# Attention and two expert layers on one core: four value blocks in place of six, queries loaded one pair of blocks later

## The chip, the cores and the metric

The kernel runs on one core of a Trainium2 chip. The core has a matmul engine (TensorE, PE in the profile; its weight loads are PEld), a vector engine (VectorE, DVE), a scalar engine (ScalarE, ACT), GpSimd (POOL) and a synchronisation engine (SyncE, SP), which here does nothing but issue DMA transfers. Sixteen DMA engines move data between the chip's DRAM and the on-chip memory SBUF. All engines run at the same time and wait for each other by semaphores.

The metric is the device time of one execution in microseconds (us), lower is better. Before the change it is 724.68 us, the median of three runs (722.94 to 727.16).

## The reference

Three layers follow one another. First, attention over 4 sequences of 576 tokens with 8 heads of 64; four heads see the last 32 tokens, the other four see every fourth of the last 128:

```python
rel = pos[:, None] - pos[None, :]
mask_plain = (rel >= 0) & (rel < window)                                             # window 32
mask_dil = (rel >= 0) & (rel < window * dilation) & (rel % dilation == 0)            # dilation 4
scores = np.where(masks[None], scale * np.matmul(q, k.transpose(0, 1, 3, 2)), -1e9)
attn = np.exp(scores - np.max(scores, axis=-1, keepdims=True))
out = np.matmul(attn / (np.sum(attn, axis=-1, keepdims=True) + 1e-09), v)
```

Then a layer of 8 experts: each of the 2304 tokens goes to the expert with the largest logit, which computes `relu(x @ w1[e]) @ w2[e]`, scaled by two gates. Last, a dense layer: `h = relu(x @ w_in)`, `out = (h * h) @ w_out`.

## The kernel before, in words

The kernel has three stages on the one core. Attention takes about the first 89 us, the experts the next 260, the dense layer the rest. The change lies in attention alone.

Attention goes over 18 blocks of 128 tokens. For each block it multiplies queries and keys into scores (`qk`, matmuls of line 454), adds the mask and takes the maximum on VectorE (lines 468 and 474), subtracts it on GpSimd (line 475), takes the exponential on ScalarE (line 480), transposes the result on PE (`tr`, line 487), copies it (line 489), multiplies it with the values (`pv`, line 503), normalises on VectorE (lines 513 to 521) and transposes the block for the gate's logits (`xt`, line 540). Blocks are gathered in five groups; at a group's end its logits and its routing lists are computed (lines 563 to 672), and its rows are stored to DRAM (`x_d`, lines 531 and 534). From the eleventh block on, the lists of the first three groups are known, the largest expert is chosen, and its weights (line 141) and tokens are loaded while attention's last blocks run.

The order of the work is written out by hand. In iteration i of the loop over blocks, PE gets `tr(i)`, `qk(i + 2)`, `xt(i - 1)` and `pv(i)`, in that order, and the loads for later blocks are issued between them from SyncE. Each engine takes its instructions in program order, and so does SyncE with its DMA issues, each of which first waits for its buffer to be free (and for a semaphore that one of the eight transfers before it held).

Three kinds of input stream into attention. A load of queries (`load_q`, line 366) brings a pair of blocks into one of three buffers. A load of keys (`load_k`, line 373) brings one to three blocks into a ring of five. A load of values (`load_v`, line 383) brings a pair of blocks into a ring `vb` of VR = 6 blocks; since each load fills only every second partition of each half, the rest of a buffer is set to zero once, by `clear_v` (line 393), one half on VectorE and one on GpSimd. `clear` (line 428) sets the routing lists in DRAM to zero.

Before the loop, queries of blocks 0 to 3, keys of blocks 0 to 4 and values of blocks 0 and 1 are loaded, then queries 4 and 5 and values 2 and 3. In iteration 0, values 4 and 5 follow.

Of the kernel before, what the change touches and what calls it, by code (L numbers as in the profile page):

```python
# [25 lines left out]
NB = NT // P  # L26
# [29 lines left out]

VN = 16 * (D + 1)
VL = -(-2 * VN // 128) * 128
VR = 6
KW = (LAP + 1) * 4 * P + 3 * P  # L60


# [9 lines left out]
def attention_experts_kernel(ctx: ExitStack, tc: tile.TileContext, qB, kB, vB, wE, wF, consts, late, rows, out):  # L72
    nc = tc.nc
# [43 lines left out]
    def loaded(ap, engine, n, why):  # L117
        _, vals = nc.values_load_multi_w_load_instructions(
            ap, engines=[engine], min_val=0, max_val=n, skip_runtime_bounds_check_because=why
        )  # L120
        return vals
# [17 lines left out]
    def load_w(r, c, queue="e"):  # L139
        t = raw_tile()  # L140
        QUEUE[queue].dma_start(out=t, in_=wE[ds(reg[queue, r], 1), c].rearrange("a p n -> p (a n)"))
        raw_t[r, c] = t

    def conv_h(r, c):
        w_t[r, c] = free.pop(0)
        nc.scalar.copy(out=slots[w_t[r, c]][:, 0], in_=raw_t[r, c])  # L146
# [22 lines left out]
    def gather(w):  # L169
        known = (NB if w else EARLY) * P  # L170
        for i, n in tiles(w):
            t = stg.tile([P, DM], F32, tag="xg", name="xg", bufs=4)
            nc.gpsimd.indirect_dma_start(  # L173
                out=t[:n], out_offset=None, in_=x_d[0:known],
                in_offset=bass.IndirectOffsetOnAxis(ap=mt[:n, w, i, 0:1].bitcast(U32), axis=0),
                bounds_check=known - 1, oob_is_err=False,
            )
            xg_t[w, i] = t
# [164 lines left out]
    def attention():  # L343
# [9 lines left out]
        kz = kf[:, :, 0:(LAP + 1) * 4 * P].rearrange("p h (t a s) -> p h t a s", t=LAP + 1, a=4)  # L353
        vb = c2.tile([P, 2, VR, 4, 4, D + 1], F32, name="vb")
        q_t = {}
# [7 lines left out]
        def load_q(i, n):  # L363
            q = wk.tile([P, 2, 4, P], F32, tag="q", name="q", bufs=3)
            a = i % 2
            nc.sync.dma_start(out=q[:, 0:n].rearrange("p i a s -> p (i a s)"), in_=qB[i // 2, :, a:a + n].rearrange("p i s -> p (i s)"))
            for j in range(n):
                q_t[i + j] = q[:, j]

        def load_k(i, n, engine=nc.sync):  # L370
            t = i % LAP
            for h2 in range(2):
                engine.dma_start(out=kf[h2:P:2, h2, 4 * P * (t + 1):4 * P * (t + 1 + n)], in_=kB[h2, :, 4 * P * i:4 * P * (i + n)])

        def wrap():

            nc.scalar.copy(out=kz[:, :, 0, 0:2, 96:P], in_=kz[:, :, LAP, 0:2, 96:P])
            nc.scalar.copy(out=kz[:, :, 0, 2:4], in_=kz[:, :, LAP, 2:4])

        def load_v(i, n, engine=nc.sync):  # L380
            j = i % VR
            for h2 in range(2):
                engine.dma_start(
                    out=vb[h2:P:2, h2, j:j + n].rearrange("p i a c e -> p (i a c e)"),
                    in_=vB[i // 2, h2, :, VN * (i % 2):VN * (i % 2 + n)],
                )
# [5 lines left out]
        def clear_v(j, h2, engine):  # L392
            engine.memset(vb[:, h2, j], 0.0)
# [27 lines left out]
        def load_consts():  # L421
            nc.sync.dma_start(out=late_sb, in_=late)
            nc.sync.dma_start(out=rowc, in_=rows)
# [3 lines left out]
        def clear():  # L427
            nc.sync.dma_start(
                out=meta_d.rearrange("(p a n) c -> p a (n c)", p=P, a=4), in_=z.unsqueeze(1).to_broadcast([P, 4, MS * E * MR // P // 4])
            )  # L430
# [6 lines left out]
        def qk(i):  # L437
            qk_mm(i)
            qk_x(i)
# [37 lines left out]
        def ex(i):  # L477

            pr = wk.tile([P, 4, 64, 2], F32, tag="pr", name="pr")
            nc.scalar.activation(out=pr.rearrange("p a m h -> p a h m"), in_=sm_t.pop(i).rearrange("p (a h) m -> p a h m", h=2), func=ACTF.Exp, scale=0.125)  # L480
            p_t[i] = pr

        def tr(i):
            pr = p_t.pop(i)
            ps = ps_1.tile([P, 4, P], F32, tag="pt", name="pt")
            for p in range(4):
                nc.tensor.transpose(ps[:, p, :], pr[:, p].rearrange("p m h -> p (m h)"), ident)
            pt = wk.tile([P, 4, P], F32, tag="pts", name="pts")
            nc.scalar.copy(out=pt, in_=ps)
            pt_t[i] = pt  # L490

        def pv_mm(i, apart=False):
# [4 lines left out]
            else:  # L497
                t = ps_1.tile([P, 4, 256], F32, tag="o", name="o")
                o = [t[:, 0:2], t[:, 2:4]]
            v = vb[:, :, i % VR]  # L500
            for p in range(4):
# [166 lines left out]
        def scatter(g, cols=None):  # L668
            di, m, _ = rt[g]
            n = rows_of(g)  # L670
            for b in cols or range(COLS[g]):
                ins = nc.gpsimd.indirect_dma_start(
                    out=meta_d, out_offset=bass.IndirectOffsetOnAxis(ap=di[n, b:b + 1].bitcast(U32), axis=0),
                    in_=m[n, b, :], in_offset=None, bounds_check=E * MS - 1, oob_is_err=False,
                ).ins
                for o in scat:
                    tc.declare_no_dep(ins, o, reason="each slot of a list is written once")
                scat.append(ins)
# [8 lines left out]
        nc.gpsimd.memset(z.rearrange("p (n c) -> p n c", c=MR)[:, :, 2:3], OOB)  # L687
        nc.gpsimd.memset(idw, 0)
        ex(0)
        load_q(4, 2)  # L690
        load_v(2, 2)
        warm(7)
        ends = {g[-1] + 1: n for n, g in enumerate(GROUPS)}
# [14 lines left out]
        for i in range(NB):  # L708
            tr(i)
            if i + 1 < NB:  # L710
                ex(i + 1)
            if i == NB - 3:
                gather(0)
            if i + 2 < NB:
                qk(i + 2)
            t = (i + 2) % LAP
            n = i + 2 - t + LAP
            if t == 2 and n < NB:
                load_k(n, 2)
            if t == 4 and n + 2 < NB:  # L720
                wrap()
                load_k(n + 2, min(3, NB - n - 2))

            if i % 2 == 0 and i + 6 < NB:
                load_q(i + 6, 2)
            if i == 0:
                load_consts()
            if i == 3:
                clear()
            if i == 3:  # L730
                nc.vector.tensor_copy(tri, tri32)
                nc.vector.tensor_copy(idw[:, :, :, 0:4], idsb)
                nc.vector.tensor_copy(cs[:, 0, :], io8)
            for a, g in ((2, ends.get(i - 2)), (4, ends.get(i - 3))):
                if g is not None and g < FIRST:
                    scatter(g, range(a - 2, min(a, COLS[g])))
            if i == EARLY + 2:
                reg["e", 0] = loaded(e0_t, SPE, E - 1, PERM)[0]
                load_w(0, 0)
                meta_load(0, nc.sync, "e")  # L740
                load_w(0, 1)
            if i == EARLY + 3:
                load_w(0, 2)
            if i > 0:
                xt(i - 1)
            if i == NB - 3:
                conv_h(0, 0)
            if i == NB - 1:
                transposes0()
            g = ends.get(i - 1)  # L750
            if g == FIRST:
                cnt = route4(g)
            pv_mm(i)
            if g is not None and g != FIRST:
                route4(g)
            if i == NB - 1:
                route5(NG - 2)
                scatter(NG - 2)
                route6(NG - 2)
                splits0()  # L760
                lg_block(i - 1)
            pv_x(i)
            if i == NB - 2:
                scale(0)
            if i == NB - 1:
                conv_w(0, 1)
            if i == 0:
                for j in range(4, VR):
                    clear_v(j, 0, nc.vector)
                    clear_v(j, 1, nc.gpsimd)  # L770
                load_v(4, 2)
            if i % 2 == 1 and i + VR - 1 < NB:
                load_v(i + VR - 1, 2)
            if i in STORES:
                store(STORES[i])
            if i in ends:
                lg(ends[i])
                route1(ends[i])
                route2(ends[i])
                route3(ends[i])  # L780
            if i == NB - 3:
                conv_l(0, 0)
                load_w(0, 3)
            if g is not None and g < NG - 2:
                route5(g)
                if g == FIRST:
                    scatter(g)
                    choose(wk, cnt)
                route6(g)
                if g == FIRST:  # L790
                    first_part(wk)
            if i == NB - 2:
                lg_block(i - 1)
                store(NG - 2)
# [889 lines left out]
```

## Time and profile before

| | before |
|---|---|
| median of 3 runs | 724.68 us (722.94 to 727.16) |
| the profiled execution | 724.47 us, span 722.8 us |
| PE busy | 694.7 us, 96% of the span |
| VectorE, ScalarE, GpSimd busy | 486.4, 326.5, 114.5 us |
| granted clock of PE | 0.998 of full speed |

The span is the time from the first to the last instruction; a little lies around it. Busy times are of one profiled execution. Idle time of an engine is put down to whatever ended it: another engine's instruction, a DMA, or "issue", where the engine waited for nothing that the profile shows.

### The profile page before, as it was taken

Reading aid. Unit: us, or ns where it says so; the run is one execution under the profiler, and the core shown is the slowest. Engines: PE = TensorE matmul, PEld = TensorE weight load, DVE = VectorE, ACT = ScalarE, POOL = GpSimd, SP = SyncE. Lnnn points to the kernel's source line nnn. Section 1 sums busy time; section 2 is a strip of 40 time slices with the busy share of each in tenths; the row PEclk is TensorE's granted clock in tenths of the full one; section 3 lists DMA queues with packets and bytes.
Section 4 is the critical chain, followed back from the end, with each engine's and each line's share of the span. In section 5 each row is a group of like instructions: output and inputs, shape, how many; then the busy total and the mean of one; then the engine's idle time right before and its main releaser. Section 6 shows DMA issues by size and latency. Waiting matters only on the chain.

```text
span 722.8 us, 13818 instructions
## 1 busy us (share of the span) xinstructions
PE 694.7 (96%) x5203; PEld 631.9 (87%) x5203; DVE 486.4 (67%) x878; ACT 326.5 (45%) x599; POOL 114.5 (16%) x120
## 2 busy tenths in 40 slices
PE   7988889999999999989999999999999999999995
PEld 4766789999999999989999999999988888888884
DVE  7866775773646567668886878787889854445441
ACT  2443544543455555556555545565534422122120
POOL 6245336202010110008000000000000040012003
PEclk9999999999999999999999999999999999999999
DMA  8999556865475776862657545556755453235302
GB/s 281 414 338 316 183 165 210 261 182 162 157 221 158 229 239 190 245 203 64 219 165 249 194 152 195 193 203 231 238 170 196 139 177 108 91 119 162 110 22 91
DMA packets 65503, 138.11 MB, mean 191 GB/s; under 512 B 12838, under 2 KB 40023, under 8 KB 64407
## 3 DMA queue, kind: packets, MB, share of 16 engines
q1 hardware_dynamic: 53538, 121.60, 51.9%
q0 software_dynamic: 3984, 10.22, 4.1%
q10 hardware_dynamic: 7909, 5.35, 2.3%
q8 instruction: 43, 0.70, 0.4%
q14 instruction: 29, 0.24, 0.1%
HBM read 102.06 MB, written 35.12 MB: 190 GB/s over the span
## 4 chain that ended last, share of the span: by engine, by line
PE 68%; issue 10%; DVE 2%; DMA 2%; POOL 1%; ACT 1%; ACTq 0%; POOLq 0%; DVEq 0%; SPq 0%
PE op L1489 6%; PE op L1490 6%; PE op L1491 6%; PE bank_b L881 5%; PE bank_b L879 4%; PE bank_b L880 4%; PE yp L879 4%; PE yp L880 4%; PE hp L879 4%; PE yp L881 4%; PE hp L880 4%; PE hp L881 4%; PE bank_d L881 2%; PE bank_d L880 2%; PE bank_d L879 2%
## 5 line engine op out<-in xcount | busy, mean ns | idle before, releaser
L1454 DVE TENSOR_TENSOR slot_d<-gq,slot_d 128x768 fp32r<-128x768 f32 x48 | 45.9, 957 | 63.8 <-ACT slot_d L1452 62.3
L1452 ACT CAST slot_d<-gq 128x768 fp32r<-128x768 f32 x48 | 40.0, 835 | 95.2 <-PE op L1490 83.1
L1499 POOL DMA_INDIRECT out<-os,idc x18 | 20.0, 1112 | 352.9 <-DVE os L1498 348.3
L893 ACT ACTIVATE hh<-hp 128x240 fp32r<-128x240 f32 (+5 forms) x72 | 29.2, 410 | 42.3 <-PE hp L881 40.4
L1445 DVE SCALAR_TENSOR_TENSOR gq<-gq 128x768 f32<-128x768 f32 x48 | 45.7, 952 | 2.1 <-DMA gq<-g_d 2.1
L173 POOL DMA_INDIRECT xg<-x_d,mt x24 | 25.7, 1069 | 135.2 <-PE xp L197 123.2
L150 DVE TENSOR_TENSOR slot_d<-raw,slot_d 128x1024 fp32r<-128x1024 f32 x24 | 29.2, 1223 | 20.6 <-ACT slot_d L146 20.1
L1489 PE MATMUL op<-slot_b,slot_d 128*128 128x512 f32 x108 | 42.0, 389 | 0.0
L1490 PE MATMUL op<-slot_b,slot_d 128*128 128x512 f32 x108 | 42.0, 389 | 0.0
L1489 PE MATMUL op<-slot_a,slot_d 128*128 128x512 f32 x108 | 42.0, 389 | 0.0
L1490 PE MATMUL op<-slot_a,slot_d 128*128 128x512 f32 x108 | 42.0, 389 | 0.0
L1491 PE MATMUL op<-slot_a,slot_d 128*128 128x512 f32 x108 | 42.0, 389 | 0.0
L1491 PE MATMUL op<-slot_b,slot_d 128*128 128x512 f32 x108 | 42.0, 389 | 0.0
L894 DVE SCALAR_TENSOR_TENSOR hl<-hp,hh 128x240 fp32r<-128x240 f32 (+5 forms) x72 | 31.5, 449 | 14.8 <-ACT hh L893 12.1
L914 ACT COPY ys<-yp 128x240 f32<-128x240 f32 (+5 forms) x36 | 14.4, 399 | 48.8 <-PE yp L881 42.5
L880 PE MATMUL yp<-hl,slot_b 128*128 128x240 f32 (+3 forms) x112 | 31.8, 284 | 0.3 <-DVE hl L894 0.3
L879 PE MATMUL yp<-hh,slot_b 128*128 128x240 f32 (+3 forms) x112 | 32.1, 286 | 0.0
L150 DVE TENSOR_TENSOR slot_b<-raw,slot_b 128x1024 fp32r<-128x1024 f32 x20 | 24.2, 1220 | 11.4 <-ACT slot_b L146 11.0
L881 PE MATMUL yp<-hh,slot_b 128*128 128x240 f32 (+3 forms) x112 | 31.7, 283 | 0.0
L879 PE MATMUL hp<-xh,slot_d 128*128 128x432 f32 (+3 forms) x96 | 30.5, 318 | 0.3 <-DVE hl L894 0.3
L880 PE MATMUL hp<-xl,slot_d 128*128 128x432 f32 (+3 forms) x96 | 30.2, 315 | 0.0
L881 PE MATMUL hp<-xh,slot_d 128*128 128x432 f32 (+3 forms) x96 | 30.2, 314 | 0.0
(338 smaller groups left out, 2277.5 us busy)
## 6 DMA issues: line engine op xcount, KB each, us to landing
raw<-in_wE SPq DMA_DIRECT2D x64, 512.0 KB
g_d<-cr SPq DMA_DIRECT2D x96, 192.0 KB
gq<-g_d SPq DMA_DIRECT2D x48, 384.0 KB
raw<-in_wF SPq DMA_DIRECT2D x32, 512.0 KB
vb<-in_vB SPq DMA_DIRECT2D x16, 520.0 KB
yr<-yT_d SPq DMA_DIRECT2D x16, 384.0 KB
q<-in_qB SPq DMA_DIRECT2D x8, 512.0 KB
kf<-in_kB SPq DMA_DIRECT2D x8, 256.0 KB
```

Of the source, the lines that this page charges most:

```text
L150: nc.vector.tensor_tensor(out=lo, in0=raw_t.pop((r, c)), in1=hi.bitcast(F32), op=ALU.subtract)
L879: nc.tensor.matmul(out=out, lhsT=wh, rhs=mh, start=first, stop=False, skip_group_check=shared)
L880: nc.tensor.matmul(out=out, lhsT=wh, rhs=ml, start=False, stop=False, skip_group_check=shared)
L881: nc.tensor.matmul(out=out, lhsT=wl, rhs=mh, start=False, stop=last, skip_group_check=shared)
L893: nc.scalar.activation(out=h[:, :n], in_=p[:, :n], func=ACTF.Relu)
L894: nc.vector.scalar_tensor_tensor(out=l[:, :n], in0=p[:, :n], scalar=0.0, in1=h[:, :n].bitcast(F32), op0=ALU.max, op1=ALU.subtract)
L1445: nc.vector.scalar_tensor_tensor(out=x, in0=x, scalar=0.0, in1=x, op0=ALU.max, op1=ALU.mult)
L1452: nc.scalar.copy(out=h, in_=x)
L1454: return lambda: nc.vector.tensor_tensor(out=l, in0=x, in1=h.bitcast(F32), op=ALU.subtract)
L1489: nc.tensor.matmul(out=o_t[j], lhsT=h[:, a], rhs=w[:, 0], start=f == 0, stop=False)
L1490: nc.tensor.matmul(out=o_t[j], lhsT=h[:, a], rhs=w[:, 1], start=False, stop=False)
L1491: nc.tensor.matmul(out=o_t[j], lhsT=l[:, a], rhs=w[:, 0], start=False, stop=f == 15)
```

## The change

The ring of values holds four blocks in place of six. Values 4 and 5 are no longer loaded in iteration 0 into buffers of their own, whose four clearing memsets go; they come in iteration 1 into the buffers of blocks 0 and 1. Every later pair of values comes in the same iteration as a pair did before, but it is the pair before that one, and one more load stands in iteration 13 (values 16 and 17). Queries go the same way: the load ahead of the loop goes, iteration i (even) loads the pair from i + 4 in place of i + 6, and iteration 12 has one more load (queries 16 and 17).

```diff
-VR = 6
+VR = 4
...
         ex(0)
-        load_q(4, 2)
         load_v(2, 2)
         warm(7)
...
-            if i % 2 == 0 and i + 6 < NB:
-                load_q(i + 6, 2)
+            if i % 2 == 0 and i + 4 < NB:
+                load_q(i + 4, 2)
...
-            if i == 0:
-                for j in range(4, VR):
-                    clear_v(j, 0, nc.vector)
-                    clear_v(j, 1, nc.gpsimd)
-                load_v(4, 2)
             if i % 2 == 1 and i + VR - 1 < NB:
                 load_v(i + VR - 1, 2)
```

The order of SyncE's issues at the start of the loop, before (`q` queries, `vb` values, `kf` keys, `late_sb` and `rowc` constants; partitions x elements of 4 bytes, `x2` two transfers):

```order
L383 DMA vb<-in_vB 64x1040 x2
L366 DMA q<-in_qB 128x1024
L383 DMA vb<-in_vB 64x2080 x2
L373 DMA kf<-in_kB 64x1024 x2
L366 DMA q<-in_qB 128x1024
L422 DMA late_sb<-in_late 128x400
L423 DMA rowc<-in_rows 1x128
L383 DMA vb<-in_vB 64x2080 x4
```

The same place after the change:

```order
L383 DMA vb<-in_vB 64x1040 x2
L383 DMA vb<-in_vB 64x2080 x2
L373 DMA kf<-in_kB 64x1024 x2
L366 DMA q<-in_qB 128x1024
L422 DMA late_sb<-in_late 128x400
L423 DMA rowc<-in_rows 1x128
L383 DMA vb<-in_vB 64x2080 x2
L373 DMA kf<-in_kB 64x1536 x2
L366 DMA q<-in_qB 128x1024
```

The first query load of the loop, which holds blocks 6 and 7 before, holds 4 and 5 after, and it is the only load of these two blocks; one pair of values is left out of the line, and keys 7 to 9 and queries 6 and 7 follow it.

SyncE's issues around iterations 12 and 13 after the change, as the difference to before (`raw` weights of the first expert, `x_d` the store of a group, `ISA` a register instruction):

```order
 L383 DMA vb<-in_vB 64x2080 x2
 L373 DMA kf<-in_kB 64x512 x2
+L366 DMA q<-in_qB 128x1024
 L531 DMA x_d<-x 128x3x256
 L534 DMA x_d<-x 32x3x256 x4
@@ -47,4 +47,5 @@
 L141 ISA
 L141 DMA raw<-in_wE 128x1024
+L383 DMA vb<-in_vB 64x2080 x2
 L141 ISA
 L141 DMA raw<-in_wE 128x1024
```

The added queries stand ahead of the third group's store, and the added values between the second and third weight loads. On PE nothing moves; on VectorE and GpSimd only the memsets of line 393 after block 0 are gone.

## Rows read from the trace of the kernel before

**Rows 1.** The first page: busy us of PE; DMA engines' busy tenths in 40 slices.
```profile
PE 694.7 (96%) x5203; PEld 631.9 (87%) x5203; DVE 486.4 (67%) x878; ACT 326.5 (45%) x599; POOL 114.5 (16%) x120
...
DMA  8999556865475776862657545556755453235302
```

**Rows 2.** Chain of waits, its beginning: start us, us, what.
```profile
102.64 0.97 POOL meta_d L672
...
110.37 4.69 DMA xg<-x_d,mt
...
115.70 0.32 PE xp L197
```

**Rows 3.** Timeline of PE, 0 to 40: start, us, instruction, count [idle before].
```profile
7.66 1.08 PE L454 MATMUL s<-kf,q 128*32 128x128 f32 x32 [0.56 <-DMA q<-in_qB]
...
11.78 0.63 PE L487 MATMUL pt<-ident,pr 128*128 128x128 f32 x4 [1.42 <-DMA ident<-in_consts]
...
13.60 1.09 PE L503 MATMUL o<-vb,pts 128*32 128x130 f32 x32 [0.18 <-DMA vb<-in_vB]
...
19.17 1.08 PE L454 MATMUL s<-kf,q 128*32 128x128 f32 x32
...
26.01 1.08 PE L454 MATMUL s<-kf,q 128*32 128x128 f32 x32
...
31.28 1.08 PE L454 MATMUL s<-kf,q 128*32 128x128 f32 x32 [0.36 <-DMA kf<-in_kB]
...
38.20 1.05 PE L503 MATMUL o<-vb,pts 128*32 128x130 f32 x26 [1.52 <-issue]
```

**Rows 4.** Timeline of SyncE's issues, 0 to 23 us.
```profile
4.07 0.59 SPq L366 DMA_DIRECT2D q<-in_qB  x1
...
6.96 0.43 SPq L410 DMA_DIRECT2D ident<-in_consts  x1
...
15.77 1.35 SPq L366 DMA_DIRECT2D q<-in_qB  x1
...
22.06 1.48 SPq L373 DMA_DIRECT2D kf<-in_kB  x2
```

**Rows 5.** DMA issues by line, with KB each.
```profile
vb<-in_vB SPq DMA_DIRECT2D x16, 520.0 KB
q<-in_qB SPq DMA_DIRECT2D x8, 512.0 KB
...
kf<-in_kB SPq DMA_DIRECT2D x8, 256.0 KB
```

**Rows 6.** Windows: us, PE busy (instructions), PE's clock, DMA share, GB/s.
```profile
13.60:31.28 17.68, 15.86 (x356) 1.00 1.02 407
...
36.00:38.00 2.00, 0.69 (x9) 1.00 1.01 400
42.00:43.00 1.00, 1.00 (x25) 1.00 0.43 164
...
43.30:61.44 18.14, 16.91 (x377) 1.00 0.98 335
61.44:69.46 8.02, 7.29 (x151) 1.00 1.00 326
77.00:82.00 5.00, 4.23 (x76) 1.00 0.81 296
```

**Rows 7.** Timeline of VectorE and GpSimd: the memsets of iteration 0.
```profile
16.10 1.87 POOL L393 MEMSET vb<- 128x1040 f32 x2
16.17 0.93 DVE L393 MEMSET vb<- 128x1040 f32 x1 [0.17 <-issue]
```

**Rows 8.** Timeline of PE, 61 to 89 us.
```profile
61.44 0.91 PE L454 MATMUL s<-kf,q 128*32 128x128 f32 x23
...
69.46 0.41 PE L454 MATMUL s<-kf,q 128*32 128x128 f32 x5
...
82.91 1.09 PE L503 MATMUL o<-vb,pts 128*32 128x130 f32 x32 [0.69 <-ACT pts L489]
...
88.97 0.38 PE L879 MATMUL hp<-xh,slot_a 128*128 128x240 f32 x1
```

**Rows 9.** Timeline of SyncE, the second and third weight load.
```profile
75.57 0.88 SPq L141 DMA_DIRECT2D raw<-in_wE  x2
```

## The prediction

> **What bounds the kernel now.** The first page says that the matmul engine is the bound: PE is busy 96% of the span, in every slice but the first and last, while the DMA engines are full only in the first slices and fall to half later [rows 1]. The chain of waits comes next. It begins where attention's last lists leave for DRAM, and runs through the gather of the first expert's tokens into that expert's transposes on PE [rows 2]. So what attention loses is not made up behind it: experts and feed-forward work on attention's tokens, and PE has 4% of idle time in all. A delay of PE inside attention is passed on whole unless attention itself has an idle stretch that takes it.
>
> The timeline of PE then shows what attention's blocks wait for [rows 3]. In four places a load ended PE's idle time: 0.56 us for the second block's queries, 1.42 for the identity, 0.18 for the first values, 0.36 for keys at 31.28. Otherwise one block follows the other. Issue times of those loads are in the DMA queue's timeline [rows 4]: queries issued at 4.07 let PE go at 7.66, 3.6 us later; the identity, 64 KB, took 6.96 to 11.78, 4.8 us; keys issued at 22.06 let PE go at 31.28, 9.2 us. The same kind of transfer takes 3.6 to 9.2 us because all of SyncE's loads stand in one line, and from 13.60 to 31.28 that line is full (DMA share 1.02, 407 GB/s) [rows 6]. How long a load takes is therefore a question of how many bytes are ahead of it, and the change alters that.
>
> **The change, part by part.** *Four memsets* of value blocks 4 and 5 go, two on VectorE (0.93 us each) and two on GpSimd (1.87 together) [rows 7]. They lie beside PE's work of block 1, and PE's next steps end on none of them: taken at nothing, at most their 1.9 us if the mask of block 3 were what PE waits for, which no row of PE shows.
>
> *Queries 4 and 5.* Before, they are issued ahead of values 2-3 and keys 5-6; after, behind both (the order of SyncE's rows). The old issue of 15.77 [rows 4], the first behind those keys, is the new one's place. What counts is the line: when PE starts on the first values at 13.60, the transfers behind them are, after the change, keys 3-4 (512 KB), values 1 (520), values 2-3 (1040), keys 5-6 (512), and then queries 4-5 (512): 3096 KB or 3.17 MB (sizes in [rows 5] and by the shapes in SyncE's rows). The rate can be calibrated in the same place: before, keys 7-9 end a line of 6656 KB (6.82 MB) from 13.60 and let PE go at 31.28, so 6.82 MB / 17.68 us = 0.386 MB/us of such loads, out of the 0.407 that the window shows. At 0.386 the queries are there at 13.60 + 8.2 = 21.8. The check: before, 1544 KB stand up to queries 4-5, 4.1 us, so 17.7, and PE's scores of block 4 start at 19.17 without a wait [rows 3]. After, they wait until 21.8: **+2.6 us**. Bounds by the rows: the shortest latency seen, 15.77 + 3.6 = 19.4, gives +0.2; the longest, 15.77 + 9.2 = 25.0, gives +5.8. I take 2.6, the count of bytes, since it also gives the absent wait of before.
>
> The Trainium skill has a formula that speaks for less: "DMA: Bandwidth & Descriptors", section "Anatomy of one DMA", puts a DMA at about 2.0 us plus its bytes over 436 GB/s. By it the queries would take 3.2 us and land at 19.0, and the term would be nothing. The identity's row disagrees (4.8 us where the formula gives 2.2), since the formula has nobody ahead in the line.
>
> *Queries 6 and 7* come behind values 4-5 and keys 7-9: 5616 KB, 5.75 MB, at 13.60 + 14.9 = 28.5. PE wants them at 26.01 before, at 28.6 with the shift of 2.6. They are just in time; a second wait here replaces the first one where PE tries to catch up, it does not add to it. So nothing, 0 to 0.5.
>
> *Keys 7-9* gain: values 6-7 and queries 6-7 no longer stand ahead of them. 5104 KB end at 27.1, long before 31.28 + 2.6. The wait of 0.36 goes: **-0.36**. What is late next there is nothing but the block's own chain.
>
> *Queries 14 and 15* take the place of 16 and 17 in block 10, and are wanted two blocks earlier, by the scores that start at 61.44 [rows 8]. The line is half empty at 42 to 43 (share 0.43); behind it come keys 12-14, values, queries, the first group's store (1024 KB), values, keys, and these queries: 5408 KB, 5.54 MB. At the window's 0.335 MB/us [rows 6], or 0.318 with the loss found above, that is 16.5 to 17.4 us from 43.3: 59.8 to 60.7. In time by about 1 us, or 0.5 late if the stores run slower.
>
> *Queries 16 and 17* become one more load (512 KB) in block 12, behind the second store, values 14-15 and key 17: 2832 KB, 2.90 MB at 0.326 from 60.7, 8.9 us, 69.6, against 69.46 for the scores that use them. That matmul group was itself broken up by idles of issue in before, from 69.46 on (its first five are in [rows 8]), so part of a wait would be hidden. For both together I take **+0.2**, bounds 0 and 1.6.
>
> *Values 16 and 17* move from block 11 to block 13, and there behind two weight loads that wait for the choice of expert: SyncE issues them at 75.57 to 76.4 [rows 9], and the values would follow at 76.1 to 77.3, between the two. 512 + 1040 KB from 77 at no less than 0.296 MB/us [rows 6] are 5.4 us, 82.4; PE wants them at 82.91 and waits there for ScalarE today. Nothing, up to 1 us late. What is queued behind them is the third weight part, which is used only in the experts.
>
> *Instruction loads.* PE stood 1.52 us at 38.20 with nothing that it waits for in the program [rows 3], in a stretch where the DMA engines were full [rows 6]. The change leaves 1.5 MB less in the line there, so this may shrink, and others, in stretches that become fuller, may grow. Nothing, from -1.5 to +1.
>
> Sum: +2.6 - 0.36 + 0.2 = +2.4. The profiled execution took 724.47, 0.21 below the runs' median of 724.68; so 726.9 for it, and **727.0** as the forecast.
>
> **The rivals.** *In time.* The line empties faster than counted and queries 4-5 land at the shortest latency: +0.2 - 0.36, so 724.3. For it: keys 7-9 made PE wait only 0.36 us before, so the line was never far behind. Against it: 13.60 to 31.28 without a gap in the DMA share.
>
> *Faster by a lighter line.* As the case before, and 1.5 MB less before 38 us also frees the instruction loads: 724.47 + 0.2 - 0.36 - 1.52 = 722.8. It decides if queries 4-5 land by 19.2. Against it: reordering inside a full line gains nothing for what is put last.
>
> *Later than two blocks at more places.* Queries now have a lead of two blocks, 5 to 8 us where the line is full, and latencies of up to 9.2 stand in the trace. Then the waits at blocks 14 and 16 and the values of 16 come at their bounds: 724.47 + 2.6 - 0.36 + 1.6 + 1 = 729.3; the first wait alone at its bound of 5.8 gives 729.9. For it: the two counts that end within 1 us of the need.
>
> *The gap lowers PE's clock.* The granted clock is 1.00, so 2.4 GHz, even in 36 to 38 us where PE was busy 0.69 of 2 us [rows 6]; its longest idle of rows 3 is 1.52, and 2.6 would be longer. Two blocks of PE's work lie between 19.17 and 26.01 [rows 3]; if the one behind the gap ran at 1.2 GHz, its 3.4 us would be had twice: 724.47 + 2.4 + 3.4 = 730.3. The Trainium skill ("TensorE: Matmul & The Clock Gate", section "Part 1: The HAM clock gate") says that an idle PE falls to the lower level and regains the higher by being busy; no run here shows it yet.
>
> **How the numbers follow.** The forecast (725.6 to 728.2) 0.53; in time 0.14; faster 0.06; later at more places 0.22; clock 0.05. What a measurement of this kernel can tell from no change is about 0.5%, 3.6 us: below 721.1, and above 728.3. Above lie nearly all of the last two cases and a little of the forecast's tail, 0.26; below only the edge of the faster case, 0.03; between, 0.71. From 723.8 to 730.0 lie the forecast, the case in time and most of the later one.
>
> **What would show it.** Right: in the profile after, PE's scores of block 4 idle 2 us or more, ended by a DMA of queries, near 21.8; the same group of block 6 with no wait or a short one; no wait for keys near 34; attention's end, the first expert matmul at 88.97 before [rows 8], some 2.4 us later, and the rest in step. Wrong: scores of block 4 that start by 19.4, a wait for queries over 1 us at a second place, a granted clock below 1.00 behind 22 us, or a first expert matmul not later than 89.

## The result, and the profile after

The changed kernel takes 730.57 us (median of 8 runs, 728.02 to 736.13); the kernel before, run beside it, 723.25 (8 runs). The ratio is 1.0108, with a 95% interval of 1.0081 to 1.0135: some 7.8 us slower (the medians lie 7.3 apart), where the prediction had +2.4. The forecast of 727.0 was 3.6 us too low, and its range ended at 730.0. (Its sum gives 726.9 for the profiled execution and 727.1 for the median; 727.0 lies between.) That the change costs time was right; that it stays within about 0.5% was not.

The profiled execution took 736.13 us and is the longest of the eight, so its sizes lie above the typical ones. What happens in it, and in which order, is read here; what each thing is worth is taken from the timed experiments.

PE's timeline answers to [rows 3, 8] (start us, us, instruction, count, idle before and what ended it):

```profile
18.02 0.66 PE L487 MATMUL pt<-ident,pr 128*128 128x128 f32 x4
22.69 1.94 PE L454 MATMUL s<-kf,q 128*32 128x128 f32 x32 [4.02 <-DMA q<-in_qB]
24.55 1.12 PE L540 MATMUL xt<-ident,x 128*128 128x128 f32 x4
25.60 1.96 PE L503 MATMUL o<-vb,pts 128*32 128x130 f32 x32
27.50 1.12 PE L487 MATMUL pt<-ident,pr 128*128 128x128 f32 x4
28.54 1.08 PE L454 MATMUL s<-kf,q 128*32 128x128 f32 x32
...
32.54 1.08 PE L454 MATMUL s<-kf,q 128*32 128x128 f32 x32 [0.72 <-DMA q<-in_qB]
...
49.17 1.94 PE L454 MATMUL s<-kf,q 128*32 128x128 f32 x32 [2.54 <-DMA q<-in_qB]
...
68.29 1.07 PE L454 MATMUL s<-kf,q 128*32 128x128 f32 x30 [2.26 <-DMA q<-in_qB]
...
71.88 1.96 PE L503 MATMUL o<-vb,pts 128*32 128x130 f32 x32
...
90.52 1.96 PE L503 MATMUL o<-vb,pts 128*32 128x130 f32 x32 [3.10 <-DMA vb<-in_vB]
...
100.85 0.36 PE L873 MATMUL hp<-xh,slot_a 128*128 128x240 f32 x1
```

Not one wait but five: for queries 4-5 (4.02 us), 6-7 (0.72), 10-11 (2.54), 14-15 (2.26) and for values 16-17 (3.10), together 12.64 us. And behind four of these waits PE is slow: 32 score matmuls take 1.94 us at 22.69 and at 49.17 and 1.08 at full clock, 32 matmuls with the values 1.96 at 71.88 and at 90.52 and 1.09 at full clock. The four groups from 22.69 on take 1.94 + 1.12 + 1.96 + 1.12 = 6.14 us, the same four at full clock 1.08 + 0.66 + 1.09 + 0.66 = 3.49.

The windows show why (us, then for PE, PEld, DVE, ACT and POOL the busy us and instructions, PE's clock, DMA share, GB/s):

```profile
16.00:18.00 2.00, 1.85 (x48) 1.24 (x36) 1.73 (x3) 1.20 (x3) 0.56 (x2) 1.00 0.94 330
18.00:20.00 2.00, 0.67 (x8) 0.42 (x4) 1.06 (x3) 1.23 (x4) 0.99 (x1) 1.00 0.98 382
20.00:22.00 2.00, 0.00 (x0) 0.00 (x0) 0.00 (x0) 0.60 (x2) 0.00 (x0) 0.94 1.07 413
22.00:24.00 2.00, 1.31 (x28) 1.22 (x32) 0.00 (x0) 0.00 (x0) 0.00 (x0) 0.50 0.80 326
24.00:26.00 2.00, 2.00 (x24) 1.27 (x20) 1.20 (x2) 0.29 (x2) 0.00 (x0) 0.50 0.13 45
...
28.00:30.00 2.00, 2.00 (x39) 1.44 (x37) 0.96 (x3) 1.17 (x2) 0.00 (x0) 0.86 0.94 301
...
98.00:100.00 2.00, 2.00 (x34) 1.52 (x26) 1.15 (x4) 1.28 (x4) 1.69 (x2) 0.50 0.02 4
...
2.26:100.85 98.59, 82.31 (x1498) 62.65 (x1499) 65.58 (x193) 37.77 (x90) 39.91 (x45) 0.86 0.83 281
```

The granted clock falls to 0.50, so 1.2 GHz, during the wait, stays there while PE is busy again, and comes back between 28 and 30 us. The longest slow stretch stands behind the last wait: from 90.52 to the first expert matmul at 100.85 it is 10.33 us, where before needed 88.97 - 82.91 = 6.06 for the same work [rows 8]. The last row is attention up to the first expert matmul. The same stretch of before, with the same instructions but for a few records:

```profile
2.26:88.97 86.71, 75.67 (x1499) 54.60 (x1499) 64.50 (x191) 36.20 (x88) 40.33 (x45) 1.00 0.88 313
```

It is 98.59 - 86.71 = 11.88 us longer, 6.64 of it busier (82.31 - 75.67) at a mean clock of 0.86, and 5.24 more idle: the five waits, less 7.4 us of idles of before that are gone. Of these, 4.6 are idles of issue (5.4 us in before, 0.8 after; the 1.52 us at 38.20 [rows 3] among them). Behind it, nothing comes back: the span grew by 734.3 - 722.8 = 11.5.

SyncE's issues of these queries in the changed kernel:

```profile
16.44 0.58 SPq L366 DMA_DIRECT2D q<-in_qB  x1
...
25.88 0.59 SPq L366 DMA_DIRECT2D q<-in_qB  x1
...
40.79 0.59 SPq L366 DMA_DIRECT2D q<-in_qB  x1
...
60.93 0.59 SPq L366 DMA_DIRECT2D q<-in_qB  x1
...
83.25 1.13 SPq L383 DMA_DIRECT2D vb<-in_vB  x2
```

From issue to use (22.69, 32.54, 49.17, 68.29, 90.52) these are 6.3, 6.7, 8.4, 7.4 and 7.3 us. The page's rows of DMA issues put the median at the same size (KB, us to landing):

```profile
vb<-in_vB SPq DMA_DIRECT2D x16, 520.0 KB, 6.6
...
q<-in_qB SPq DMA_DIRECT2D x8, 512.0 KB, 6.6
```

PE would have wanted queries 10-11 at 49.17 - 2.54 = 46.63, 5.8 us after their issue, and queries 14-15 at 66.03, 5.1 after it. A lead of 5 to 6 us stands against a landing of 6.6. The prediction put these two numbers side by side only in a rival (a lead of 5 to 8 us, latencies of up to 9.2), not in its sum.

### The profile page after: what moved, and what is told of

Its sections match the earlier page's. It is cut to its first block, busy times and chain, and to the rows that moved or that the text cites. A ratio compares the mean times of both kernels' runs of the same rounds, so it can differ in the third digit from the quotient of the medians.

```text
span 734.3 us, 13811 instructions
## 1 busy us (share of the span) xinstructions
PE 702.5 (96%) x5203; PEld 641.2 (87%) x5203; DVE 485.1 (66%) x876; ACT 326.7 (44%) x599; POOL 113.2 (15%) x118
## 5 line engine op out<-in xcount | busy, mean ns | idle before, releaser
L454 PE MATMUL s<-kf,q 128*32 128x128 f32 x576 | 23.4, 310 | 10.4 <-DMA q<-in_qB 9.5
L150 DVE TENSOR_TENSOR slot_b<-raw,slot_b 128x1024 fp32r<-128x1024 f32 x20 | 24.2, 1219 | 11.5 <-ACT slot_b L146 11.1
L873 PE MATMUL hp<-xh,slot_d 128*128 128x432 f32 (+3 forms) x96 | 30.5, 318 | 0.3 <-DVE hl L888 0.3
L454 PEld LDWEIGHTS s<-kf,q 128*32 128x32 f32 x576 | 17.6, 124 | 15.1 <-DMA q<-in_qB 7.7
```

The lines of the kernel that those rows point to most:

```text
L150: nc.vector.tensor_tensor(out=lo, in0=raw_t.pop((r, c)), in1=hi.bitcast(F32), op=ALU.subtract)
L454: nc.tensor.matmul(out=s[32 * c:32 * c + 32, 2 * p:2 * p + 2, :], lhsT=q[:, p, 32 * c:32 * c + 32], rhs=rhs, start=True, stop=True)
L873: nc.tensor.matmul(out=out, lhsT=wh, rhs=mh, start=first, stop=False, skip_group_check=shared)
```

## The experiments

Each was timed beside the kernel before on its chip, 6 to 12 runs. The ratio is to that kernel, with its interval, and 0.001 is 0.73 us. The clock is the mean over the runs; for before it is 0.993 to 0.994 throughout, and for the changed kernel 0.985.

**The two halves.** Queries only:

```
-        load_q(4, 2)                      (ahead of the loop)
-            if i % 2 == 0 and i + 6 < NB: load_q(i + 6, 2)
+            if i % 2 == 0 and i + 4 < NB: load_q(i + 4, 2)
```

> Six value blocks as before; queries loaded as after the change. Theory Q (most of the loss is the late queries: waits of 4.0, 2.5 and 2.3 us at blocks 4, 10 and 14 in the profile after, each followed by matmuls at half clock): the three waits stay, the wait for values at block 16 is gone; about two thirds of the loss of 7.3 us, so 728 (ratio to before 1.006). Rival V (the values' wait at the end costs most): 724.5, within 0.2% of before.

Values only: VR = 4 and the values' loads as changed, queries as before.

> Four value blocks as after; queries loaded as before. Theory Q: only the wait for values 16 and 17 at about 82 to 90 us is left (3.1 us in the profile after, and half clock behind it): 725.5 to 726.5 (ratio 1.003 to 1.0045). Rival V: 728 or more (1.007). If four value blocks cost nothing at all, as a lighter line early on would have it: 723.

Queries only: 1.0095 [1.0064, 1.0126], clock 0.988. Values only: 1.0055 [1.0029, 1.0081], clock 0.989. Each half costs, and together (1.0108) less than their sum of 1.0150. Rival V, which had the queries within 0.2%, is refuted; they cost more than theory Q's 1.006 too. Of the waits that theory Q took from the changed kernel's profile, the first is there with queries only (4.06 us at 22.46), but those of 2.54 and 2.26 us are not:

```profile
47.55 1.08 PE L454 MATMUL s<-kf,q 128*32 128x128 f32 x32 [0.47 <-DMA q<-in_qB]
...
65.84 1.07 PE L454 MATMUL s<-kf,q 128*32 128x128 f32 x29 [0.19 <-DMA q<-in_qB]
```

In the kernel with values 16-17 ahead of the weights (below), which is the changed one up to iteration 13, they are 0.49 and 1.29, and the first 4.17. So the first wait repeats from trace to trace, and the sizes of the later ones do not. In the values-only kernel one place in PE's timeline stands out:

```profile
77.94 0.66 PE L487 MATMUL pt<-ident,pr 128*128 128x128 f32 x4
...
83.07 1.96 PE L503 MATMUL o<-vb,pts 128*32 128x130 f32 x32 [3.91 <-DMA vb<-in_vB]
...
91.94 0.36 PE L874 MATMUL hp<-xh,slot_a 128*128 128x240 f32 x1
```

Block 16 starts at 77.94 (80.77 in before), waits 3.91 us for its values, and goes on at half clock. Since block 16 came 2.8 us sooner, the wait itself loses almost nothing in these two traces: the product with the values starts at 83.07 against 82.91 [rows 8]. What is lost comes behind it, at half clock: the first expert matmul stands at 91.94 against 88.97.

**Filler in the waits.** The changed kernel with matmuls that compute nothing used, put where PE waits, except ahead of blocks 6 and 7:

```
+                if i in {2: 14, 8: 8, 12: 8}: warm(...)   (ahead of qk(i + 2))
+            if i == NB - 2: fill(10)                      (ahead of its pv)
```

> The kernel after, with matmuls that nothing reads put into the four gaps of PE: 14 of 128x512 bf16 ahead of the scores of block 4, 8 ahead of those of 10 and of 14, 10 ahead of the product with values of block 16 (about 0.24 us each, shorter than the gaps). Theory C (about half of the loss is the half clock behind each gap): waits end when they ended, the granted clock stays at 1.00, 726 (ratio to before 1.004). Rival W (only the waits count, and PE has slack behind them): no change, 730.5 (1.010); or slower, 732, if the added matmuls hold up PE.

1.0119 [1.0082, 1.0157]: nothing won. The clock held behind 22 us, and the scores of block 5 started 3.3 us sooner (25.24 against 28.54). The next wait, 0.72 us without filler, took half of that: those of block 6 started 1.6 us sooner (30.95 against 32.54).

```profile
22.04 1.08 PE L462 MATMUL s<-kf,q 128*32 128x128 f32 x32 [0.36 <-DMA q<-in_qB]
...
30.95 1.08 PE L462 MATMUL s<-kf,q 128*32 128x128 f32 x32 [2.42 <-DMA q<-in_qB]
```

**Values 16-17 ahead of the weights.** The changed kernel, with the first expert's loads moved behind the load of these values.

> The kernel after, with the load of values 16 and 17 issued ahead of the first two weight loads of the chosen expert and not behind them. Theory: the wait for values at block 16 (3.1 us) and the half clock behind it go, 3 to 4 us of the median's 7.3: 727 (ratio 1.005). Rival: the weights and the list, now behind the values, are what the end of attention waits for next, so the end comes no sooner: 730.

1.0122 [1.0084, 1.0160]: nothing won, as the rival had it. The wait for values was gone, and the list of the first expert's tokens became late instead. GpSimd, which gathers the tokens by that list, waited 5.48 us for it, so its step of block 17 (line 475) came late, and with it the exponential on ScalarE and the matmuls of PE behind that. (The profiled execution, 738.04 us, is the longest of six.)

```profile
83.53 1.24 POOL L173 DMA_INDIRECT xg<-x_d,mt  x1 [5.48 <-DMA mt<-meta_d]
...
87.19 0.67 ACT L480 ACTIVATE pr<-sm 128x512 f32<-128x512 f32 x1 [4.42 <-POOL sm L475]
...
88.16 1.89 PE L571 MATMUL lg<-late_sb,xT 128*128 128x16 f32 x8 [4.00 <-ACT xT L542]
```

**The first wait alone, without and with filler.** The kernel before, queries 4-5 loaded in iteration 0:

```
-        load_q(4, 2)            (ahead of the loop)
+            if i == 0: load_q(4, 2)
+                if i == 2: warm(14)     (only in the second kernel)
```

> The kernel before, with only its load of queries 4 and 5 moved from ahead of the loop to iteration 0, behind keys 5 and 6 (queries 6 and 7 right behind it). So the first wait alone, everything later as before. Theory G (this first wait is worth several us by itself: about 4 us of idle, 2.7 us of blocks at half clock behind it, some 2 us given back at the next idle stretch): 727 to 728, ratio 1.005 to 1.0065. Rival A (later idle takes nearly all of it): 724.3, ratio 1.0015.

> As the one-gap kernel, with 14 filler matmuls on PE ahead of the scores of block 4, in the idle stretch of the wait. Theory C (the half clock behind the wait is a cost of its own): scores start as without filler, the clock stays at 1.00, the transposes of block 3 start about 2.7 us sooner, and the time is 725, ratio 1.0025. Rival W (the next wait takes back what the clock gives): the same time as unfilled within 0.8 us.

1.0025 [1.0006, 1.0045], clock 0.992; with filler 1.0009 [0.9989, 1.0029], clock 0.995. So this wait is worth 1.8 us by itself: theory G (at least 1.005) is ruled out, rival A's 1.0015 is not. In the trace it is 3.91 us long, and the half clock behind it costs another 2.6, as in the changed kernel. What its trace gives back is the idle of issue that stood at 38.20 [rows 3], 1.52 us. That run took 731.63 us, 2.5 above the median, and its first expert matmul is 5.2 us late; what gives back the rest in the other runs is not seen. The filler moved the transposes of block 3 from 27.45 to 24.82, 2.6 us as expected; the two intervals overlap, so its 1.2 us in time are not shown by this pair.

```profile
17.91 3.18 PE L361 MATMUL warm<-ones 128*128 128x512 bf16 x14
22.19 1.08 PE L454 MATMUL s<-kf,q 128*32 128x128 f32 x32 [1.10 <-DMA q<-in_qB]
...
24.82 0.66 PE L487 MATMUL pt<-ident,pr 128*128 128x128 f32 x4
```

**Everything but the first wait.** The changed kernel with `load_q(4, 2)` back ahead of the loop; and the kernel before with queries 6 and later two blocks closer.

> The changed kernel with its load of queries 4 and 5 put back ahead of the loop; all else as changed (four value buffers, two blocks of lead for the other queries). Theory G (the first wait is a large single part): 726, ratio 1.004. Rival L (a lead of two blocks is too short everywhere, so the later waits come all the same): 729.5, ratio 1.009.

> The kernel before, with queries 6 and later loaded two blocks closer to their use; queries 4 and 5 stay ahead of the loop, and six value buffers stay. Theory G (the first wait is what costs): 724, ratio 1.001. Rival L (the lead of two blocks costs at every pair): 727 or more, ratio 1.005.

1.0047 [1.0028, 1.0065] and 1.0074 [1.0050, 1.0099]. The two answers differ. In the changed kernel theory G holds and rival L is refuted: this one load, put back, saves 4.4 us (1.0108 to 1.0047, intervals apart), more than twice what its wait costs alone. In the kernel before theory G is refuted: 5.4 us are lost without the first wait. In both the wait for queries 6-7 took its place, 3.56 us in the first kernel and 6.36 in the second, which still has values 6-7 ahead of them in the line, besides 4-5:

```profile
32.70 1.94 PE L454 MATMUL s<-kf,q 128*32 128x128 f32 x32 [6.36 <-DMA q<-in_qB]
```

So what a load's wait is worth depends on what else is late, and the parts do not add up.

**Which queries.** The kernel before, with the later place (`i + 4`) only for queries from 8, 10 or 14 on:

```
+            if i % 2 == 0 and i + 6 < FROM: load_q(i + 6, 2)
+            if i % 2 == 0 and FROM <= i + 4 < NB: load_q(i + 4, 2)
```

> The kernel before, with only the queries of blocks 8 and later loaded two blocks closer to their use. Theory L (a lead of two blocks costs also where the line of loads is not full): 1.003 to 1.004. Rival E (only the two early waits, at blocks 4 and 6, cost; later ones fall into idle time that is there anyway): 1.000 to 1.001.

> The kernel before, with only queries of blocks 10 and later two blocks closer. Theory F (the waits come from the backlog of the line of loads, which is full up to about 40 us; behind that, two blocks are enough): 1.000 to 1.002, no wait for queries over 1 us. Rival H (the first pair that is moved waits wherever it stands, and puts PE behind for the rest): a wait of 2 to 4 us at block 10, ratio 1.005 or more.

> The kernel before, with only queries 14 to 17 loaded two blocks closer to their use: the very term that the prediction put at 0.2 us. Theory P (that count of bytes holds, they are just in time): 1.000 to 1.001. Rival T (they cost by themselves, as those from block 8 on did): 1.004.

From 8: 1.0074 [1.0050, 1.0098], more than either expected. From 10: 1.0022 [1.0004, 1.0040]. From 14: 1.0002 [0.9987, 1.0017], as theory P had it. The pair 8-9 is the one that costs most here: it is issued at 26.63 into a line that is full to 40 us, PE starts on it 11.4 us later, and goes on at half clock. The wait and the windows of the kernel from 8 on (columns as above):

```profile
37.98 1.08 PE L454 MATMUL s<-kf,q 128*32 128x128 f32 x32 [3.37 <-DMA q<-in_qB]
...
36.00:38.00 2.00, 0.02 (x3) 0.02 (x3) 0.42 (x4) 0.67 (x2) 0.00 (x0) 1.00 1.04 412
38.00:40.00 2.00, 2.00 (x40) 1.47 (x44) 0.77 (x2) 0.00 (x0) 0.00 (x0) 0.79 1.00 415
40.00:42.00 2.00, 2.00 (x34) 1.49 (x34) 0.65 (x2) 0.65 (x2) 1.07 (x2) 0.50 0.68 271
```

From 10 on, the first moved pair waits 0.85 us, not 2 to 4: the backlog up to 40 us decides the most (theory F), and rival H is refuted. But theory F had no wait over 1 us, and the last pair has one, with half clock behind it (a granted clock of 0.63 at 74 to 76 us). What is left costs 1.6 us.

```profile
72.47 0.86 PE L454 MATMUL s<-kf,q 128*32 128x128 f32 x19 [1.68 <-DMA q<-in_qB]
```

**Three blocks of lead.** The kernel before, queries 6 and later in odd iterations (`load_q(i + 5, 2)`).

> The kernel before, with queries 6 and later loaded in odd iterations, so that their lead is three blocks, between the four of before and the two of the changed kernel; queries 4 and 5 stay ahead of the loop, six value buffers. Theory L (the lead in time decides; three blocks, some 10 us, cover nearly all latencies seen, which go to 11.4): 1.000 to 1.002. Rival B (any place further back in the full line costs): 1.004 or more.

1.0020 [1.0001, 1.0039], clock 0.994, no wait for queries over 0.7 us in the trace from block 2 on (the keys of block 7 wait 1.31). Against the 1.0074 of the same queries with two blocks of lead, most of the loss goes with one more block, as theory L had it.

**Half clock, a cost of its own?** The kernel with late queries from 8 on, and 14 filler matmuls ahead of block 8's scores.

> As the kernel with queries from block 8 on two blocks closer (1.0074), with 14 filler matmuls on PE ahead of the scores of block 8, in the idle stretch of 3.4 us. Theory C (half clock behind the wait costs by itself): the clock stays at 1.00 behind 38 us, and the time is 2 to 2.7 us less, ratio 1.004. Rival W (the next waits take it back): 1.007.

1.0012 [0.9995, 1.0029], clock 0.995, against 1.0074 and 0.990 without (on another chip, each beside the kernel before on its own): the intervals are apart. Rival W is refuted, and theory C holds in that the half clock is a cost of its own; its size, 2 to 2.7 us saved, is too small. PE computes the scores at the same time (38.03 against 37.98), and only the pace behind them differs; the windows that answer to those just shown:

```profile
38.00:40.00 2.00, 2.00 (x52) 1.61 (x55) 0.72 (x2) 0.27 (x1) 0.00 (x0) 1.00 1.02 423
40.00:42.00 2.00, 2.00 (x60) 1.63 (x53) 1.72 (x4) 0.98 (x4) 1.04 (x1) 1.00 0.68 273
```

The 4.5 us saved are more than the two traces show (the first expert matmul 92.21 against 94.07 us); where the rest lies is open.

**The values without their last wait.** Four blocks in the ring for blocks 0 to 15, and two buffers of their own for 16 and 17, loaded in iteration 11 as before; with queries as before, and in the changed kernel:

```
-            j = i % VR
+            j = i % VR if i < NB - 2 else i - NB + 2 + VR
+            if i == 11: load_v(NB - 2, 2)
```

> The kernel before with a ring of four value blocks for blocks 0 to 15, and two buffers of their own for blocks 16 and 17, loaded in iteration 11 as before; queries as before. So the values part of the change without its wait at block 16. Theory V (that one wait is all that the smaller ring costs; with values only, the blocks stood 2.9 us ahead of the kernel before just ahead of it): 0.997 to 1.000. Rival R (the later loads of the other values cost by themselves): 1.004 or more, as with values only (1.0055).

> The changed kernel with two buffers of their own for the values of blocks 16 and 17, loaded in iteration 11; queries two blocks closer, as changed. Theory S (the wait for those values, 3.1 us and the half clock behind it, is a part of the loss of its own): 1.006 to 1.007. Rival N (the time is lost at the next wait, as it was where these values went ahead of the weights): 1.010.

0.9996 [0.9975, 1.0016] and 1.0075 [1.0049, 1.0102]. Theory V holds: loading the values of blocks 4 to 15 later costs nothing, and the wait at block 16 is all that the smaller ring costs. (The clearing memsets that the change drops stand in these two kernels, for the two extra buffers.) In the changed kernel that wait's part is 1.0108 - 1.0075, some 2.4 us (theory S, though the intervals overlap).

**The identity sooner.** As the first of these two, with the identity ahead of queries 2-3.

> As the kernel with two value buffers of their own, and the identity loaded ahead of queries 2 and 3, not behind them, so that PE's wait of 1.4 to 2.1 us at about 12 us shrinks. Theory T (PE is the bound behind it, so what is won there stays): 1 to 1.5 us less than without, ratio 0.995 to 0.998. Rival Q (the full line of loads sets the pace up to 31 us, so a later wait takes it): as without, within 0.5 us.

0.9998 [0.9971, 1.0024]: the wait at 11.8 us for the identity became one of 1.03 us for ScalarE, and no time is won: rival Q's size, though the interval takes in the upper end of theory T (0.998), and which later wait takes the gain is not shown. No version here beats the kernel before.

**Filler, with the values in time.**

> As the changed kernel with two value buffers of their own (1.0075), with filler matmuls on PE in the idle stretches ahead of the scores of block 4 (14) and block 6 (6). Theory C (with the wait at block 16 gone, what the clock loses behind the early waits is saved for good): mean clock of the runs 0.992 or more in place of 0.988, ratio 1.003 to 1.004. Rival W (the early waits for queries grow by what the clock gives, as they did in the filled changed kernel): 1.007.

1.0084 [1.0052, 1.0116], against 1.0075 without filler: rival W, and theory C's 1.003 to 1.004 is refuted. The waits for queries are still there at six blocks. Ahead of block 4 filler and wait take 3.19 + 1.71 = 4.90 us (4.83 without filler), ahead of block 6 1.46 + 1.05 = 2.51 (1.62 without):

```profile
18.57 3.19 PE L361 MATMUL warm<-ones 128*128 128x512 bf16 x14
23.47 1.08 PE L454 MATMUL s<-kf,q 128*32 128x128 f32 x32 [1.71 <-DMA q<-in_qB]
...
32.30 1.08 PE L454 MATMUL s<-kf,q 128*32 128x128 f32 x32 [1.05 <-DMA q<-in_qB]
...
79.75 1.93 PE L454 MATMUL s<-kf,q 128*32 128x128 f32 x32 [1.47 <-DMA q<-in_qB]
```

With all queries late, PE seems to go at the pace at which they land, so that a faster clock only makes it wait longer. That would reconcile the two outcomes: filler pays where a single wait has slack behind it (late from 8 on), and not where the next load is late as well. It is inferred from the wait ahead of block 6, here and in the filled changed kernel, and not tried by itself.

## Why the prediction was wrong

The step that failed is the sum: it priced one late load, and put the queries of blocks 8 to 13 at nothing without a reason, the values of blocks 16 and 17 at nothing by a count, and the clock into a rival of 0.05. The runs show a cost in each of the three. Two of the prediction's own signs of being wrong came: a wait for queries over 1 us at a second place (2.54), and a granted clock below 1.00 behind 22 us.

- *What bounds the kernel*: right. In the profiled executions attention's delay was passed on whole (11.9 us at the first expert matmul, 11.5 in the span).
- *Queries 4 and 5, +2.6*: the mechanism was right, the place too (22.69 against 21.8). That the wait by itself is worth 1.8 us, near the 2.6 - 0.36 = 2.2 that the sum had for it with the keys, is luck, since errors cancelled. The wait was 4.02 us, not 2.6: PE got to it sooner (18.67, not 19.17), and the line of 3.17 MB ran at 3.17 / (22.69 - 13.59) = 0.348 MB/us, not 0.386 (330 GB/s at 16 to 18 us). The half clock added 2.65. Against that, much was given back later, of which one trace shows 1.5 us. And in the changed kernel the same load is worth 4.4 us, twice the term; why more than by itself is open. The formula that the prediction weighed against its count is given there (the Trainium skill, "DMA: Bandwidth & Descriptors", section "Anatomy of one DMA") for transfers that GpSimd issues, and these are SyncE's. The trace bears its 3.2 us out as little: from issue to use it shows 6.3 (16.44 to 22.69).
- *Queries 6 and 7, nothing*: nearly right in the changed kernel (0.72 us, bound 0.5; 0.75 to 1.62 in three other traces with all queries late), but only because the first wait stood ahead of it.
- *Queries 8 to 13*: not counted at all. The text went from block 6 to block 14. By themselves the queries from 8 on cost 5.4 us, 3.8 of them the pair 8-9 (1.0074 - 1.0022). This is the first step that failed. In the changed kernel PE is late already when it comes to block 8, and the wait shows at block 10; what these queries cost there was not measured by itself.
- *Queries 14 to 17, +0.2*: the count holds where they alone are late (+0.1 us, -0.9 to +1.2). In the changed kernel's profile 14-15 waited 2.26 us, with queries only 0.19. The count took a line in which bytes queue without a gap; in fact SyncE issues a load only when PE has come to its block (DMA share 0.13 at 24 to 26 us, behind the first wait), so every block that PE does faster shortens the lead.
- *Values 16 and 17, "nothing, up to 1 us late"*: the second step that failed, 3.10 us in the profile, 4.0 us of time by themselves, some 2.4 in the changed kernel. 5.4 us to landing were set against a lead of 5.9 (77 to 82.91). In the profile 7.3 came (83.25 to 90.52) against a lead of 4.2 (PE was there at 87.42); by themselves 8.1 (74.97 to 83.07) against 4.2.
- *The memsets and the other values, nothing*: right for the values (0.9996); the memsets alone were not tried.
- *Instruction loads, nothing, -1.5 to +1*: in the profile PE's idles of issue in attention fell by 4.6 us, beyond the bound, while PE waited for loads elsewhere. That an emptier line did it is not shown.
- *The clock*, a rival with a chance of 0.05 and one stretch of 3.4 us: the third step. It was true four times in one execution, and filler in one wait saved 4.5 us at the same start of the scores. Over the runs, the mean clock is 0.985 against 0.993. The Trainium skill ("TensorE: Matmul & The Clock Gate", section "Part 1: The HAM clock gate") has PE fall to the lower level when it is idle and regain the higher by work, and the windows agree (0.50 at 22 to 26 us, behind an idle of 4.02; 0.86 at 28 to 30, with PE busy from 22.69 on). The prediction weighed it against 36 to 38 us of before [rows 6], whose one idle is 1.52 us, and had no row of an idle of 2.6.
- *The chances*: "later than two blocks at more places" (0.22) was the case that came, along with the clock. The forecast treated these as alternatives; they belong together, since a wait can also cost the clock, and each is a chance of its own.

## What to carry to other kernels

When a load moves closer to its use, put two numbers side by side for every load of that stream, not for the first: the time from its issue to its use (the blocks between, at the pace that the engine has when it waits for nothing), and the time to landing that the DMA rows show in that stretch. Where the first is the smaller, a lightly filled line does not help. Price an idle of PE of the sizes seen here (2 to 6 us) with the work at half clock that may stand behind it, and look for the idle further on that gives time back: the first wait, 3.91 us long, cost 1.8 us by itself; the values' wait, as long, 4.0; the wait for the pair 8-9, 3.37 us long, 3.8. And do not add such prices up: the first load was worth 1.8 us alone and 4.4 in the changed kernel.

## What was not expected of the hardware

The clock does not follow the length of an idle alone. In the kernel with queries late from 14 on, a wait of 1.84 us was followed by half clock:

```profile
12.27 0.63 PE L487 MATMUL pt<-ident,pr 128*128 128x128 f32 x4 [1.84 <-DMA ident<-in_consts]
12.82 1.33 PE L454 MATMUL s<-kf,q 128*32 128x128 f32 x32
13.91 1.98 PE L503 MATMUL o<-vb,pts 128*32 128x130 f32 x32
```

In the filled changed kernel the wait of 2.42 us at 30.95, shown above, was not followed by it: its scores took 1.08 us, and the next two groups ran at full clock as well:

```profile
31.96 0.66 PE L548 MATMUL xt<-ident,x 128*128 128x128 f32 x4
32.55 1.09 PE L511 MATMUL o<-vb,pts 128*32 128x130 f32 x32
```

The runs of one and the same kernel differ by their clock too: in the 29 runs of before that stood beside the one-wait kernel (724.58 to 730.51 us), time and mean clock go together (correlation -0.74, 0.53 us for each 0.001 of clock).
